# A statically ordered gated-attention kernel: V copies on another engine, gate rows by DMA, a serial-queue model and a split last round

## The chip, the cores and the metric

The kernel runs on one core of one Trainium2 chip. The metric is the device time in microseconds (us) of one execution. The time is a little longer than the span of the profile: the execution before that was profiled has a span of 677.7 us, and the timed runs of it lie near 680.

An exponential takes the larger part of the work here, so three engines matter most: ScalarE (ACT in the profile), which computes exponentials; VectorE (DVE) and GpSimd (POOL), which together compute the same function by integer arithmetic for a share of the blocks; and TensorE (PE), which makes the scores and the products with V. SP (SyncE) is the engine that issues nearly all DMAs. PSUM is the memory that holds the results of the matmuls; the kernel uses it in banks of 512 columns.

## The reference, cut to what matters

```python
def reference(A_x, A_wqkv, A_wo, B_x, B_wqkv, B_wo, gate_w):      # S = 2048, D = 512, H = 32, Dh = 16
    x = A_x
    g = _sigmoid((x * gate_w).sum(-1, keepdims=True))
    a = _A_ref(x, A_wqkv, A_wo)     # softmax attention, 32 heads, then @ wo
    b = _B_ref(x, B_wqkv, B_wo)     # linear attention with phi(t) = elu(t) + 1, then @ wo
    return g * a + (1 - g) * b
```

Softmax attention over 32 heads of 2048 x 2048 scores, with a head size of only 16, makes 134 million exponentials. That is why the exponential, not the matmul arithmetic, sets the scale of the time.

## The kernel before

The kernel writes its instructions in an order that it computes itself while it is built. It has a list scheduler: each candidate instruction has a planned duration, a priority and a set of reads and writes; at each step the scheduler takes the best candidate, and some twenty constants ("weights") decide what is best. The result is one fixed order per engine, with semaphore waits worked out from the reads and writes. I call the length that this computation expects for its own order "the plan". It is a number of the builder, not a time.

The waits are put on an instruction in the order in which the dependencies happen to be listed:

```python
def add(self, fn, deps=(), inc=True, dma_sem=None):
    waits = []
    for d in deps:
        if d is None:
            continue
        ...                                  # keeps the highest value for each semaphore
        waits.append((sem, val))
```

The scores are 2048 blocks of 128x512. ScalarE takes two at a time (128x1024). VectorE takes single blocks by one add and clamp (`op1`), and each pair of such blocks then needs two shifted copies, on GpSimd or on VectorE:

```python
return C(AC, 500, 427 * n + 49, lambda: nc.scalar.activation(              # pair of blocks on ScalarE
    P[:, slot, 0:512 * n], bank(b0, n), ACT.Exp, scale=ESC), ...)
return C(DV, OPP, 533 * n + 74, lambda: nc.vector.tensor_scalar(o, i, ZB, 0.0, op0=ALU.add, op1=ALU.max), ...)   # op1
if E is PO and (len(dst["shifts"]) < PMIN or PO.free > DV.free + PLATE): ...  # GpSimd leaves the shift
    return C(PO, 400, 70 + 484 * n, lambda: nc.gpsimd.tensor_tensor(...), ..., f"pshift {m}")
return C(DV, ..., 69 + 134 * n, lambda: nc.vector.tensor_scalar(...), ..., f"shift {m}", lock=True)
```

How many blocks go to VectorE isn't a constant. A rule hands out one block, or two if VectorE has little queued and fewer than SHB shifts wait:

```python
got = sorted(got[:min(len(banks[:2]) if len(dst["op1"]) < 1 and DV.free < start + BACK
                      and len(dst["shifts"]) < SHB else 1, cur["todo"])])
```

The three shifted terms of such a block need V scaled by three coefficients: V itself and two scaled copies of it, made on GpSimd after VectorE has cast V out of PSUM:

```python
yield dv(607, lambda: nc.vector.tensor_copy(Vc[:, 0, vs, :, :, 0:16], src), [r_bank[b]], [r_V[vs]])
for k in range(1, NTERM):
    yield po(690, lambda k=k: nc.gpsimd.tensor_scalar(Vc[:, k, vs]..., Vc[:, 0, vs]..., COEF[k], 1.0,
                                                      op0=ALU.mult, op1=ALU.mult), [r_V[vs]], [r_V[vs]])
```

The gate is spread over partitions by four tiny VectorE copies (`dv(150, ... nc.vector.tensor_copy(gnat[32*a:32*(a+1), :], src))`). A DMA is planned as "start plus latency", whatever else its queue holds:

```python
start = max(E.free, _avail(E, reads, writes))
E.free = start + issue                # issue = 60
fin = start + lat
```

The output of each attention round is transposed, normalised, and transposed back as `OAT` in whole 128x512 pieces; after the last round the projection and four output copies follow.

The softmax here doesn't subtract the row's maximum and nothing guards it: scores larger than these inputs give would overflow.

## Time and profile before

| | before |
|---|---|
| time, median of three runs | 680.0 us (679.25 to 680.65) |
| span of the profiled execution | 677.7 us |
| ScalarE: pairs and singles of exponentials | 694 + 1 |
| first exponential starts | 9.93 us |
| last exponential starts / span ends | 668.73 / 677.71 us |
| ScalarE stalls between first and last exponential | 16.0 us |
| blocks on VectorE | 659 |
| shifts on GpSimd / on VectorE | 465 / 195 |

The stalls come from the trace by one rule: for each exponential, take the distance from its start to the start of ScalarE's next instruction, and subtract the normal step (904 ns for a pair, 477 ns for a single and for one of the 32 `phi` activations). What is left over is stall. Busy shares can't give this, because ScalarE's recorded spans overlap. The prediction below shows the profile lines themselves.

### The profile page before, as it was taken

What the parts mean: (1) busy time and instruction counts of PE and PEld (TensorE: products, weight loads), DVE (VectorE), ACT (ScalarE), POOL (GpSimd) and SP (SyncE); (2) the same over time, 40 slices, a digit from 0 to 9 for tenths busy, and PEclk for the clock granted to TensorE, in tenths of its full rate; (3) what the DMA queues carried; (4) which work ended last, traced back from release to release, by engine and by line L of the source; (5) the groups of instructions that cost most, each with busy time, mean ns of one, the idle gap of its engine ahead of it and who ended that gap; (6) DMA issues with size and microseconds to landing.
All of it is one profiled execution on the core that took longest, in us unless ns stands there. A gap on an engine that the chain in (4) does not pass through costs nothing.

```text
span 677.7 us, 24102 instructions
## 1 busy us (share of the span) xinstructions
PE 667.5 (98%) x9886; PEld 203.2 (30%) x9886; DVE 607.9 (90%) x1062; ACT 658.2 (97%) x734; POOL 550.1 (81%) x611
## 2 busy tenths in 40 slices
PE   8999999999999999999999999999999999999998
PEld 4322233323223232222333322232332332222222
DVE  6999999998899998999899888899998988899996
ACT  5899999999999999999999999999999999999995
POOL 3767878888878888888897888898788997887882
PEclk9999999999999999999999999999999999999999
DMA  6430001200000000000002000001020021000000
GB/s 133 135 89 8 4 2 35 69 9 3 2 10 1 10 2 2 10 2 2 12 3 65 10 10 1 10 18 22 7 34 9 14 48 31 17 16 11 26 17 32
DMA packets 27963, 15.96 MB, mean 24 GB/s; under 512 B 19792, under 2 KB 26832, under 8 KB 27856
## 3 DMA queue, kind: packets, MB, share of 16 engines
q1 hardware_dynamic: 26512, 13.91, 8.1%
q8 instruction: 79, 1.29, 0.8%
q10 hardware_dynamic: 1344, 0.52, 0.3%
q14 instruction: 28, 0.23, 0.1%
HBM read 6.69 MB, written 2.10 MB: 13 GB/s over the span
## 4 chain that ended last, share of the span: by engine, by line
PE 77%; ACT 13%; issue 5%; DVE 4%; DMA 0%; POOL 0%; ACTq 0%; DVEq 0%; POOLq 0%
PE ps L371 59%; PE ps L377 18%; ACT P L771 11%; DVE Z L685 2%; ACT eb L1056 1%; DMA xnat<-wA 0%; DVE T L1021 0%; DVE gnat L1013 0%; DVE QT L957 0%; DVE wA L1163 0%; PE ps L899 0%; DVE Z L749 0%; DVE OAT L1048 0%; POOL Z L739 0%; DVE rec L1040 0%
## 5 line engine op out<-in xcount | busy, mean ns | idle before, releaser
L771 ACT ACTIVATE P<-ps 128x1024 bf16<-128x1024 f32 x695 | 645.6, 1118 | 5.9 <-PE ps L371 5.8
L739 POOL TENSOR_TENSOR Z<-Z,mcon 128x512 int32<-128x512 int32 x465 | 480.0, 1056 | 81.9 <-DVE Z L685 49.4
L685 DVE TENSOR_SCALAR Z<-ps 128x512 int16<-128x512 f32 x659 | 441.2, 684 | 53.3 <-PE ps L371 45.7
L371 PE MATMUL ps<-Z,Vc 128*17 128x512 bf16 x1977 | 282.4, 382 | 0.2
L371 PE MATMUL ps<-Qz,KT 32*128 32x512 bf16 x2048 | 272.2, 384 | 3.4 <-DVE Z L685 1.0
L371 PE MATMUL ps<-P,Vc 128*17 128x512 bf16 x1389 | 250.1, 383 | 0.2
L371 PEld LDWEIGHTS ps<-Qz,KT 32*128 32x128 bf16 x2048 | 68.5, 91 | 259.1 <-ACT P L771 235.1
L371 PEld LDWEIGHTS ps<-Z,Vc 128*17 128x17 bf16 x1977 | 63.8, 88 | 79.4 <-issue 52.3
L749 DVE TENSOR_SCALAR Z<-Z 128x1024 int16<-128x1024 int16 x195 | 81.2, 433 | 0.2
L371 PEld LDWEIGHTS ps<-P,Vc 128*17 128x17 bf16 x1389 | 56.3, 88 | 55.4 <-issue 40.7
L371 PE MATMUL ps<-warm 128*32 128x512 bf16 (+15 forms) x600 | 62.5, 327 | 1.2 <-DVE dummy L420 1.2
L377 PE MATMUL ps<-xT,wA 128*32 128x512 bf16 (+1 forms) x528 | 43.9, 376 | 0.1
L1057 POOL TENSOR_SCALAR eb<-eb 128x512 f32<-128x512 f32 x32 | 20.1, 629 | 15.6 <-ACT eb L1056 9.1
L988 POOL TENSOR_SCALAR Vc<-Vc 128x576 bf16<-128x576 bf16 x32 | 21.6, 675 | 6.9 <-DVE Vc L985 3.5
L371 PEld LDWEIGHTS ps<-warm 128*32 128x32 bf16 (+1 forms) x600 | 20.3, 96 | 18.8 <-issue 12.4
L1021 DVE STREAM_TRANSPOSE T<-ps 128x512 f32<-128x512 f32 x32 | 22.6, 708 | 2.5 <-PE ps L377 2.3
L377 PE MATMUL ps<-wA,xnat 128*32 128x512 bf16 x256 | 22.6, 382 | 1.7 <-DVE wA L1163 1.7
L1044 POOL TENSOR_TENSOR T<-T,rg 128x256 bf16<-128x256 f32 x31 | 19.5, 630 | 5.7 <-DVE Z L749 2.7
L377 PE MATMUL ps<-phiK,xnat 128*32 128x512 bf16 x256 | 23.1, 383 | 0.0
L377 PE MATMUL ps<-wA,OAT 128*32 128x512 bf16 x256 | 22.5, 382 | 0.0
L1056 ACT ACTIVATE eb<-ps 128x512 f32<-128x512 f32 x32 | 22.5, 702 | 0.0
L377 PE MATMUL ps<-wB,xT 128*32 128x512 bf16 x256 | 22.4, 381 | 0.0
(79 smaller groups left out, 279.2 us busy)
## 6 DMA issues: line engine op xcount, KB each, us to landing
Qz<-QT SPq DMA_DIRECT2D x120, 16.0 KB, 1.8
wA<-in_A_wqkv_dram SPq DMA_DIRECT2D x4, 384.0 KB, 4.6
wB<-in_B_wqkv_dram SPq DMA_DIRECT2D x4, 384.0 KB, 3.3
xnat<-in_A_x_dram SPq DMA_DIRECT2D x3, 512.0 KB, 3.7
out_dram<-outt SPq DMA_DIRECT2D x12, 128.0 KB, 1.7
wA<-in_A_wo_dram SPq DMA_DIRECT2D x1, 512.0 KB, 3.6
wA<-in_B_wo_dram SPq DMA_DIRECT2D x1, 512.0 KB, 4.6
out_dram<-wA SPq DMA_DIRECT2D x4, 128.0 KB, 1.8
```

The costliest lines, as they stand in the source:

```text
L371: return lambda: nc.tensor.matmul(o, lhsT=l, rhs=r, start=start, stop=stop, skip_group_check=sg)
L377: h = nc.tensor.matmul(o[32 * j:32 * j + 32], lhsT=l[:, 32 * j:32 * j + 32], rhs=r, start=start, stop=stop, skip_group_check=True)
L685: return C(DV, OPP, 533 * n + 74, lambda: nc.vector.tensor_scalar(o, i, ZB, 0.0, op0=ALU.add, op1=ALU.max), [r_bank[b] for b in bks], r_Z[ ...
L739: return C(PO, 400, 70 + 484 * n, lambda: nc.gpsimd.tensor_tensor(Z[:, z, 0:512 * n].bitcast(I32), Z[:, z0, 0:512 * n].bitcast(I32), mcon[ ...
L749: return C(DV, 450 if hot else 300, 69 + 134 * n, lambda: nc.vector.tensor_scalar(Z[:, z, 0:512 * n], Z[:, z0, 0:512 * n], float(m), None, ...
L771: return C(AC, 500, 427 * n + 49, lambda: nc.scalar.activation(P[:, slot, 0:512 * n], bank(b0, n), ACT.Exp, scale=ESC), [r_bank[b0 + k] fo ...
L988: yield po(690, lambda k=k: nc.gpsimd.tensor_scalar(Vc[:, k, vs].rearrange("p a b c -> p (a b c)"), Vc[:, 0, vs].rearrange("p a b c -> p ( ...
L1021: yield dv(607, lambda: nc.vector.transpose(T1[:, a, :], bank(7)), [r_bank[7]], [r_T1[a]])
L1044: yield E(340 if r == NR - 1 else 640, lambda k=k: (nc.vector if r == NR - 1 else nc.gpsimd).tensor_tensor(dst_[:, k], src[:, k, :, 0:16], ...
L1056: yield ac(480, lambda: nc.scalar.activation(eb[:, i, :], bank(b), ACT.Exp), [r_bank[b]], [r_eb[i]])
L1057: yield po(640, lambda: nc.gpsimd.tensor_scalar(eb[:, i, :], eb[:, i, :], 1.0 + 1e-6, 0.0, op0=ALU.min, op1=ALU.max), [r_eb[i]], [r_eb[i]])
```

## The change

The intent is to shift load between VectorE and GpSimd, to take small delays off single places, and to make the plan agree better with the chip, with the weights searched anew for the new plan. The core of it, cut:

```diff
@@ add: the wait expected last is placed first
-        for d in deps:
-            if d is None:
-                continue
+        for d in sorted([d for d in deps if d is not None], key=lambda d: -d.fin if isinstance(d, _Ev) else 0.0):
@@ weights (some of them)
-    SHB = 4
+    SHB = 3
-    PMIN = 2
+    PMIN = 1
-    SLK = 43.219
+    SLK = 88.975
...
@@ serial queue model in dma(); occ is 1100 for transposes and loads, 650 otherwise
+            if E is SP and occ:
+                q_free[0] = max(q_free[0], start) + occ
+                fin = q_free[0] - occ + lat
@@ V copies
-                yield po(690, lambda k=k: nc.gpsimd.tensor_scalar(Vc[:, k, vs]..., COEF[k], 1.0, op0=ALU.mult, op1=ALU.mult), ...)
+                yield ("OP", DV, 214, lambda k=k: nc.vector.tensor_scalar(Vc[:, k, vs]..., COEF[k], None, op0=ALU.mult), ..., True)
@@ gate rows
-                yield dv(150, lambda a=a, src=src: nc.vector.tensor_copy(gnat[32 * a:32 * (a + 1), :], src), [r_ge], [r_gnat])
+                yield ("DMA", gnat[32 * a:32 * (a + 1), :], gp[32 * a:32 * (a + 1), 16 * a:16 * (a + 1)], semGN, 64, 2500.0, ...)
@@ last round in halves of 256 columns
+            if r == NR - 1:
+                for hf in range(2):
+                    ...        # transpose, reciprocal, gate, multiply, transpose back, each on half the columns
+                    yield ("FLAG", lambda hf=hf: flags.add(("oatl", hf)))
+                return
@@ the last projections wait for their own half; three of the four last copies on ScalarE
-            yield ("WAIT", lambda: ("oat", NT8 - 1, qc) in flags)
+            yield ("WAIT", lambda: (("oatl", qbl // 2) if tail else ("oat", NT8 - 1, qc)) in flags)
-            if tail and qbl % 2 == 1:
+            if tail and qbl != 2:
```

## The prediction

> **What bounds the kernel now.** I read the page's busy line first, then the groups by line, then the start-to-start spacing of each engine's instructions in the trace, then the waits, and last the timeline around each hole of ScalarE. The busy line and five groups (line, engine, operation, names, shapes, count | busy us, mean ns | idle before, releaser):
>
> ```profile
> PE 667.5 (98%) x9886; PEld 203.2 (30%) x9886; DVE 607.9 (90%) x1062; ACT 658.2 (97%) x734; POOL 550.1 (81%) x611
> ...
> L771 ACT ACTIVATE P<-ps 128x1024 bf16<-128x1024 f32 x695 | 645.6, 1118 | 5.9 <-PE ps L371 5.8
> L739 POOL TENSOR_TENSOR Z<-Z,mcon 128x512 int32<-128x512 int32 x465 | 480.0, 1056 | 81.9 <-DVE Z L685 49.4
> L685 DVE TENSOR_SCALAR Z<-ps 128x512 int16<-128x512 f32 x659 | 441.2, 684 | 53.3 <-PE ps L371 45.7
> ...
> L749 DVE TENSOR_SCALAR Z<-Z 128x1024 int16<-128x1024 int16 x195 | 81.2, 433 | 0.2
> ...
> L988 POOL TENSOR_SCALAR Vc<-Vc 128x576 bf16<-128x576 bf16 x32 | 21.6, 675 | 6.9 <-DVE Vc L985 3.5
> ```
>
> There are 2048 score blocks of 128x512. ScalarE takes them in pairs by its exponential (694 pairs and one single: 1389 blocks). The other 659 go to VectorE (L685, one each), with one 1024-wide shift per block, 465 of them on GpSimd (L739) and 195 on VectorE (L749). Spans of ScalarE overlap (1118 ns long, yet typically 904 ns from start to start), so its 97% hides stalls. By spacing, ScalarE's floor is 694 x 0.904 + 32 x 0.477 (phi, L1056) + about 0.9 (one single, one gate) = 643.6 us. The first exponential starts at 9.9 us and the last is over at about 669.6, so 659.7 us hold 643.6 of work: **ScalarE is the bound, with 16 us of stalls, a head of 10 us and a tail of 8 us**. Time can fall only through fewer exponentials (0.904 us a pair), fewer stalls, or a shorter tail.
>
> Summing what each start-to-start step exceeds its normal step by gives where the 16 us are: 3.7 between 20 and 40 us, 0.9 at 65 us, 1.8 at 559 us, the other 9.5 or so spread thin. The timeline (start us, us, engine, instruction) names three causes:
>
> ```profile
> 22.48 1.42 POOL L988 TENSOR_SCALAR Vc<-Vc 128x576 bf16<-128x576 bf16 x2
> 24.23 0.40 PE L371 MATMUL ps<-P,Vc 128*17 128x512 bf16 x4
> 24.68 1.02 ACT L771 ACTIVATE P<-ps 128x1024 bf16<-128x1024 f32 x1 [1.42 <-PE ps L371]
> ...
> 63.12 2.13 DVE L1013 COPY gnat<-ge 32x16 f32<-32x16 f32 x4
> 66.76 1.94 ACT L771 ACTIVATE P<-ps 128x1024 bf16<-128x1024 f32 x2 [0.76 <-PE ps L371]
> ...
> 556.36 5.19 SPq L348 DMA_TRANSPOSE xnat<-wA  x3
> 559.63 0.69 DVE L1163 TENSOR_TENSOR wA<-ps,wA 128x512 bf16<-128x512 f32 x1 [2.06 <-DMA xnat<-wA]
> 561.50 1.02 ACT L771 ACTIVATE P<-ps 128x1024 bf16<-128x1024 f32 x1 [1.66 <-PE ps L371]
> ```
>
> First: PV matmuls stand behind the scaled V copies on GpSimd, and ScalarE starves. Second: four tiny gate copies, planned at 150 ns each, hold VectorE 2.13 us. Third: eight Qz copies and three transposes queue on SyncE's in-order queue, which the build-time scheduler took for independent, so VectorE stands 2.06 us at an instruction issued too early. The tail:
>
> ```profile
> 670.41 0.72 DVE L1021 STREAM_TRANSPOSE T<-ps 128x512 f32<-128x512 f32 x1 [2.27 <-PE ps L377]
> 672.12 0.71 DVE L1048 STREAM_TRANSPOSE OAT<-T 128x512 bf16<-128x512 bf16 x1
> 672.88 1.20 PEld L377 LDWEIGHTS ps<-wA,OAT 128*32 128x32 bf16 x28 [0.42 <-DVE OAT L1048]
> 674.63 0.59 ACT L1202 CAST wA<-ps 128x512 bf16<-128x512 f32 x1 [0.49 <-PE ps L377]
> ```
>
> From the accumulator's transpose to OAT is 2.4 us in series, then 2.4 us of projection and copies, then 2.5 us of output DMA.
>
> **What the Trainium skill says.** "SBUF — State Buffer", section "Who interferes with whom": VectorE in a 2-port mode and GpSimd exclude each other for a whole instruction. The trace agrees: the gate copies last 167 to 969 ns for one shape, the shifts L749 283 to 1160 ns. "VectorE: DVE Perf Modes", section "Mode 4×_2P": a bf16 tensor_scalar from SBUF to SBUF may make 4 elements a cycle. The shifts agree in slope: 434 ns for 1024 elements, 284 for 512, so 0.29 ns an element. "Perfetto Trace Analysis", section "Identifying Dependency Chains": an instruction that waits on several engines may have EventSemaphore instructions ahead of it. The trace shows them, and the wait that the source places first is the one left on the instruction. From release to start I find 51 ns on TensorE when the last release was for the instruction's own wait, 115 ns when it was for the separate one; on GpSimd (VectorE releasing) 79 against 149.
>
> **Part by part.**
>
> V copies. GpSimd loses 32 x 0.75 us (spacing) = 24.0 us. It can take 24.0 / 0.995 = 24 more shifts, worth 24 x 0.331 = 8.0 us of VectorE. VectorE gains 32 copies; from the two shift shapes one of 576 elements lasts 303 ns and, with the shifts' overlap of 103 ns, takes 0.20 us: 6.4 us. Net gain 1.6 us of VectorE, **almost a wash**. The port time is a wash too (24 us of GpSimd traded for shifts there). What remains is latency: V ready after 0.5 us instead of 1.42, off the hole at 22 to 26 us (2.2 us): I take 1.2 us.
>
> Gate rows by DMA: 2.1 us of VectorE off, and the 0.9 us hole at 65 us. Four small DMAs join the queue at about 0.7 us each (as the Qz ones do), long before the rows are first used at 449 us.
>
> VectorE work: 1.6 + 2.1 = 3.7 us freed; a block moved from ScalarE costs it 0.598 + 0.331 = 0.93, so 4 blocks, 2 exponentials, 1.8 us.
>
> Thresholds (shift queue 4 to 3, GpSimd may take a lone shift, PMIN 2 to 1, and the searched weights): GpSimd idles 81.9 us before its shifts and VectorE 53.3 us before L685. If a tenth to a fifth of GpSimd's idle turns into shifts (8 to 16), VectorE gains 2.7 to 5.3 us; with better use of its own gaps I put 8 more blocks, 4 exponentials, 3.6 us. This is a choice, not a derivation.
>
> Wait order: some 100 waits on TensorE end with a separate semaphore instruction last, 64 ns each, so 6.4 us of TensorE; some 45 on GpSimd at 70 ns, 3.2 us. Most is beside ScalarE's work. Of the thin 9.5 us I take 2.0.
>
> DMA queue model: the hole at 559 us, 1.8 us.
>
> Last round in halves: first half's OAT comes about 1.3 us after the accumulator instead of 2.4 (two 341 ns transposes as planned, small ops between), the second about 0.2 us later than now; half the projection and its copies then lie under the second half. After OAT I expect 1.2 us instead of 2.4, so net 1.0 us.
>
> Sum: 1.2 + 0.9 + 1.8 + 3.6 + 2.0 + 1.8 + 1.0 = 12.3 us. The whole order is made anew, so new accidents like those at 34, 37 and 369 us (0.3 to 0.6 us each) will come; I charge 3.3 us. 680.0 - 12.3 + 3.3 = **671 us**.
>
> **Rivals.** (a) Resource wash: ScalarE keeps about 695 exponentials and only the named holes and the tail go, less accidents: 675 to 679. For it: VectorE and GpSimd merely exchange work, TensorE has no slack to show. (b) The engines get fuller: lone shifts let GpSimd use a third of its idle time, exponentials fall by 15 to 20, and the time to 658 to 664. For it: 82 us idle on GpSimd and 53 on VectorE; against it: those gaps are mostly waits for L685 and for TensorE, so for data. (c) Port collision: 32 more 2-port operations wait up to 0.8 us each for a GpSimd shift, up to 20 us of VectorE and a time of 680 to 688; against it, the copies carry the scheduler's lock flag, unlike the gate copies.
>
> **Range and chances.** I hold (a) at 30%, the middle path at 50%, (b) at 15%, (c) at 5%. Two per cent faster is below 666.4 us: it needs (b) or a lucky middle, 0.18. Slower by 2% is above 693.6: 0.02. Range 663 to 678.
>
> **What would show it.** Right: Vc copies on VectorE near 300 ns; exponentials near 689 (count of L771); no hole above 1 us on ScalarE between 40 us and its last exponential; GpSimd shifts up by 20 or more and VectorE shifts down; separate-semaphore releases last on TensorE falling from 100 to a few tens; last OAT to last output copy near 1.2 us. Wrong: a count of L771 below 680 (then the thresholds mattered more), an unchanged count with new holes (then (a)), or Vc copies of 0.6 us and more (then (c)).

## The result and the profile after

| | before | after |
|---|---|---|
| time, median (range), 4 runs each in the same rounds | 680.33 us (679.25 to 682.12) | 676.80 us (676.61 to 677.12) |
| span of the profiled execution | 677.7 us | 674.8 us |

The ratio is 0.9946, with a 95% interval of 0.9924 to 0.9968. A ratio here is always the mean time of one kernel's fast runs over the mean of the other's fast runs of the same rounds, so it isn't quite the ratio of the medians quoted. The kernel is 3.5 us faster by the medians; the forecast was 9.0 us. The time lies inside the predicted range of 663 to 678 us, near its slow end. All outputs are right.

The page of the kernel after gives the busy line and the groups that answer to those of the prediction (line, engine, operation, names, shapes, count | busy us, mean ns | idle before, releaser):

```profile
PE 662.7 (98%) x9908; PEld 201.6 (30%) x9933; DVE 602.8 (89%) x1066; ACT 658.2 (98%) x735; POOL 556.8 (83%) x604
...
L778 ACT ACTIVATE P<-ps 128x1024 bf16<-128x1024 f32 x695 | 645.6, 1138 | 4.6 <-PE ps L377 4.3
L746 POOL TENSOR_TENSOR Z<-Z,mcon 128x512 int32<-128x512 int32 x490 | 508.0, 1061 | 82.4 <-DVE Z L692 61.1
L692 DVE TENSOR_SCALAR Z<-ps 128x512 int16<-128x512 f32 x658 | 441.7, 684 | 57.3 <-PE ps L377 51.6
...
L756 DVE TENSOR_SCALAR Z<-Z 128x1024 int16<-128x1024 int16 x168 | 69.4, 427 | 0.1
```

Its groups by line also have the weight loads of the score matmuls (PEld, which overlaps with the matmuls) and the V copies:

```profile
L377 PEld LDWEIGHTS ps<-Qz,KT 32*128 32x128 bf16 x2048 | 67.6, 90 | 262.0 <-ACT P L778 234.3 <-DVE Z L692 15.9 <-issue 5.1
...
L995 DVE TENSOR_SCALAR Vc<-Vc 128x576 bf16<-128x576 bf16 x32 | 9.9, 311 | 0.1
```

Work did move as intended: GpSimd has 25 more shifts (465 to 490), VectorE 27 fewer (195 to 168), and each V copy lasts 311 ns. But the count in L778 did not move: 695 pairs, against 694 pairs and one single. VectorE's busy time fell by 5.1 us (607.9 to 602.8), and its idle time before its block instruction rose by 4.0 us (53.3 to 57.3). The freed time became idle time.

Next, the two named holes in the timeline (start us, us, engine, instruction; a number in brackets at the end is idle time before it). Around the gate and around 559 us after the change:

```profile
59.48 7.69 ACT L778 ACTIVATE P<-ps 128x1024 bf16<-128x1024 f32 x8
62.07 2.41 SPq L358 DMA_DIRECT2D gnat<-ge  x4
```

```profile
539.32 23.19 ACT L778 ACTIVATE P<-ps 128x1024 bf16<-128x1024 f32 x25
541.41 8.07 SPq L354 DMA_TRANSPOSE xnat<-wA  x4
552.13 4.96 SPq L358 DMA_DIRECT2D Qz<-QT  x8
555.61 0.65 DVE L1190 TENSOR_TENSOR wA<-ps,wA 128x512 bf16<-128x512 f32 x1
```

ScalarE runs through both places in one unbroken row of exponentials, 8 and 25 of them. Before the change, three of the eight transposes stood behind the Qz copies in the queue, and a VectorE instruction waited for the first of these. Now six stand before the Qz copies (the four shown are the last of them) and two behind, at 557.13 and 558.99 us, but no VectorE instruction waits for those two: the last of its kind, at 555.61 us, starts without a wait.

At the start there is a new hole (timeline after):

```profile
13.95 3.03 POOL L746 TENSOR_TENSOR Z<-Z,mcon 128x512 int32<-128x512 int32 x3 [2.23 <-DVE Z L692]
15.35 0.68 DVE L992 CAST Vc<-ps 128x512 bf16<-128x512 f32 x1
17.14 0.30 DVE L995 TENSOR_SCALAR Vc<-Vc 128x576 bf16<-128x576 bf16 x1
17.30 1.04 POOL L746 TENSOR_TENSOR Z<-Z,mcon 128x512 int32<-128x512 int32 x1 [0.32 <-DVE Z L692]
18.62 0.30 DVE L995 TENSOR_SCALAR Vc<-Vc 128x576 bf16<-128x576 bf16 x1
20.03 0.60 PE L377 MATMUL ps<-P,Vc 128*17 128x512 bf16 x6
20.47 6.52 ACT L778 ACTIVATE P<-ps 128x1024 bf16<-128x1024 f32 x7 [1.88 <-PE ps L377]
```

V is cast by 16.03 us, and its two copies, 0.30 us each, are over only at 18.92 us: one starts 0.16 us after a GpSimd shift has ended (16.98), the other 0.28 us after the next one (18.34). ScalarE waits 1.88 us.

And the tail (timeline after):

```profile
667.52 0.45 DVE L1031 STREAM_TRANSPOSE T<-ps 128x256 f32<-128x256 f32 x1 [3.89 <-PE ps L377]
668.77 0.45 DVE L1059 STREAM_TRANSPOSE OAT<-T 128x256 bf16<-128x256 bf16 x1
669.14 0.41 DVE L1031 STREAM_TRANSPOSE T<-ps 128x256 f32<-128x256 f32 x1
670.35 0.45 DVE L1059 STREAM_TRANSPOSE OAT<-T 128x256 bf16<-128x256 bf16 x1
671.95 0.58 ACT L1229 CAST wA<-ps 128x512 bf16<-128x512 f32 x1 [1.15 <-PE ps L383]
```

The halves do what they say, but a half transpose takes 0.41 to 0.45 us where a whole one took 0.72, so two halves in series are longer than one whole.

The span, taken apart by the stall rule:

| part of the span (us) | before | after | predicted change | measured change |
|---|---|---|---|---|
| first exponential starts | 9.93 | 9.31 | 0 | -0.62 |
| stalls up to 40 us | 3.84 | 4.65 | -1.2 | +0.81 |
| hole at 65 us (gate copies) | 0.91 | 0 | -0.9 | -0.91 |
| hole at 559 us (queue) | 1.77 | 0 | -1.8 | -1.77 |
| other stalls | 9.5 | 9.06 | -2.0 | -0.4 |
| exponentials | 694 + 1 | 695 | -5.4 | 0 |
| last exponential's start to the end | 8.98 | 8.97 | -1.0 | -0.01 |
| "new accidents" | | | +3.3 | in the rows above |
| sum | 677.71 | 674.78 | -9.0 | -2.9 |

The kernel before ends on a single exponential and the kernel after on a pair, so the row of the tail compares unlike ends; from the start of the accumulator's first transpose to the end it is 7.30 us before and 7.26 us after, which says the same. This is one profile of each kernel, so a row below about 0.5 us is not worth much. A second profile of the same kernel after (run a_again below) has a span of 676.6 us, 1.8 us more: its first exponential starts at 9.85, and it has a hole of 1.1 us near 22 us that the first profile lacks, before which TensorE waited for DMA transposes of x. The two large rows that vanished, 65 and 559 us, are absent in both (at 545 us the second has two stalls of 0.34 and 0.26).

### The profile page after: what moved, and what is told of

Same layout as the page of the kernel before. It is cut to its first block, busy times and chain, and to the rows that moved or that the text cites. A ratio compares the mean times of both kernels' runs of the same rounds, so it can differ in the third digit from the quotient of the medians.

```text
span 674.8 us, 24186 instructions
## 1 busy us (share of the span) xinstructions
PE 662.7 (98%) x9908; PEld 201.6 (30%) x9933; DVE 602.8 (89%) x1066; ACT 658.2 (98%) x735; POOL 556.8 (83%) x604
## 4 chain that ended last, share of the span: by engine, by line
PE 48%; ACT 37%; issue 13%; DVE 1%; DMA 1%; ACTq 0%; DVEq 0%
PE ps L377 37%; ACT P L778 36%; PE ps L383 10%; ACT eb L1083 1%; DMA xnat<-wA 1%; DVE Z L692 0%; DVE T L1035 0%; ACTq L1495 0%; PE ps L906 0%; DVE wA L1190 0%; ACT wA L1229 0%; DVE T L1031 0%; DVE OAT L1059 0%; ACT KT L930 0%; DVE Z L756 0%
## 5 line engine op out<-in xcount | busy, mean ns | idle before, releaser
L778 ACT ACTIVATE P<-ps 128x1024 bf16<-128x1024 f32 x695 | 645.6, 1138 | 4.6 <-PE ps L377 4.3
L746 POOL TENSOR_TENSOR Z<-Z,mcon 128x512 int32<-128x512 int32 x490 | 508.0, 1061 | 82.4 <-DVE Z L692 61.1
L692 DVE TENSOR_SCALAR Z<-ps 128x512 int16<-128x512 f32 x658 | 441.7, 684 | 57.3 <-PE ps L377 51.6
L377 PE MATMUL ps<-Z,Vc 128*17 128x512 bf16 x1974 | 275.3, 382 | 1.7 <-DVE T L1035 1.4
L377 PE MATMUL ps<-P,Vc 128*17 128x512 bf16 x1390 | 244.2, 383 | 0.0
L377 PEld LDWEIGHTS ps<-Qz,KT 32*128 32x128 bf16 x2048 | 67.6, 90 | 262.0 <-ACT P L778 234.3
L377 PEld LDWEIGHTS ps<-Z,Vc 128*17 128x17 bf16 x1974 | 61.4, 88 | 76.1 <-issue 50.4
L377 PEld LDWEIGHTS ps<-P,Vc 128*17 128x17 bf16 x1390 | 54.3, 88 | 55.5 <-issue 45.1
L756 DVE TENSOR_SCALAR Z<-Z 128x1024 int16<-128x1024 int16 x168 | 69.4, 427 | 0.1
L377 PE MATMUL ps<-warm 128*32 128x512 bf16 (+14 forms) x624 | 60.0, 327 | 4.6 <-issue 3.2
L383 PE MATMUL ps<-xT,wB 128*32 128x512 bf16 x256 | 22.0, 382 | 0.0
```

The source lines that it names most:

```text
L377: return lambda: nc.tensor.matmul(o, lhsT=l, rhs=r, start=start, stop=stop, skip_group_check=sg)
L383: h = nc.tensor.matmul(o[32 * j:32 * j + 32], lhsT=l[:, 32 * j:32 * j + 32], rhs=r, start=start, stop=stop, skip_group_check=True)
L756: return C(DV, 450 if hot else 300, 69 + 134 * n, lambda: nc.vector.tensor_scalar(Z[:, z, 0:512 * n], Z[:, z0, 0:512 * n], float(m), None, ...
```

## The experiments

Twelve kernels ran. A name that starts with b is the kernel before with something added, a is the kernel after with something undone or added, n is a new set of weights. The runs of the kernel before beside them had medians of 680.95, 680.84 and 680.75 us in the three groups.

These runs of the kernel before are of two kinds. In the first group 5 have a granted TensorE clock of 1.000 in the mean and a mean time of 680.46 us, and 6 have 0.997 and 681.34 us; in the third group 4 have 1.000 (680.29 us) and 5 have 0.997 (681.40 us). The ratios mix them. b_sort, b_halves and b_gate_same, which keep the old order, have runs at 0.997 too; every run of a kernel whose plan knows the queue has 0.999 or 1.000.

### First group: one part alone on the kernel before

**b_dma: the serial queue model alone.** The weights stay as they were; the plan makes a new order.

```diff
+            if E is SP and occ:
+                q_free[0] = max(q_free[0], start) + occ
+                fin = q_free[0] - occ + lat
...
-            yield ("DMA", dst, src, sem, 16 * n, lat, [now()], wr, False, k == 0)
+            yield ("DMA", dst, src, sem, 16 * n, lat + 1000.0, [now()], wr, False, k == 0)
```

> The kernel before with the serial DMA queue model alone, and with its own old weights; the order is made anew from about two thirds of the run on. The theory of the parts: the hole at 559 us closes, 1.8 us less, 678.5. The rival: the order that this model makes is longer in itself (its builder expects 1.1 us more than for before), so that the hole goes but no more than 0.7 us is gained, or the hole is only moved.

Measured: 678.94 us (678.64 to 679.63), ratio 0.9972 (0.9960 to 0.9983). The timeline around the old hole:

```profile
544.16 31.31 ACT L774 ACTIVATE P<-ps 128x1024 bf16<-128x1024 f32 x34
...
560.07 0.68 DVE L1166 TENSOR_TENSOR wA<-ps,wA 128x512 bf16<-128x512 f32 x1
```

The hole is gone, 34 exponentials run through it, and the time falls by about 2 us. This confirms that part: forecast 1.8 us, measured 1.9 (0.28% of 680.95). All five runs have a clock of 1.000; against the runs of the kernel before with the same clock it is 1.5 us by the means (678.99 against 680.46), so about 0.4 us of the 1.9 are the kernel before's runs at the lower clock. The new plan was in fact 1.1 us longer than the old one, and still the chip was faster: the old plan was shorter only because it didn't know of the queue.

**b_gate_same: gate rows by DMA, order unchanged.** The four VectorE copies become four memsets of one column that keep their slots in the order, and four DMAs are issued.

```diff
-                yield dv(150, lambda a=a, src=src: nc.vector.tensor_copy(gnat[32 * a:32 * (a + 1), :], src), [r_ge], [r_gnat])
+                yield dv(150, lambda a=a: nc.vector.memset(dummy[:, 0:1], 0.0), [r_ge], [r_dummy])
+            def rows():
+                for a in range(4):
+                    dma(SP, gnat[32 * a:32 * (a + 1), :], gp[32 * a:32 * (a + 1), 16 * a:16 * (a + 1)], semGN, 64, 2500.0, ...)
```

> The kernel before with the gate rows by four small DMAs alone; in the plan the four copies are replaced by four tiny memsets, so that every compute engine keeps its order. Both theories: the hole at 65 us closes (0.9 us less), time about 679.4. If the hole had another cause, it stays and the time is unchanged.

Measured: 681.07 us, ratio 1.0003 (0.9990 to 1.0016). No gain. Yet the hole at 65 us is gone from its profile. What is there instead, in that profile's timeline, lies 490 us later:

```profile
559.45 0.69 DVE L1171 TENSOR_TENSOR wA<-ps,wA 128x512 bf16<-128x512 f32 x1 [1.82 <-DMA xnat<-wA]
561.32 1.97 ACT L772 ACTIVATE P<-ps 128x1024 bf16<-128x1024 f32 x2 [1.47 <-PE ps L371]
```

Stalls of 1.59, 1.04 and 0.51 us stand at 559, 562 and 564 us where the kernel before has one of 1.77, and one of 0.82 at 503 us where it has none above 0.15. Two things other than the gate rows go into that. The stall at 503 us (a VectorE instruction that waits for a transpose) stands also in the profiles of b_dma (0.81) and b_sort (0.59), which don't have the gate edit. And the longer stalls from 559 us on go with a lower clock. From `--windows` of this run (stretch, its length, busy us of PE, PEld, DVE, ACT and POOL, then the granted clock, the DMA share and GB/s):

```profile
561.00:564.00 3.00, 3.00 (x29) 0.60 (x26) 1.70 (x3) 1.97 (x2) 1.58 (x2) 0.66 0.24 49
```

In the next 3 us the mean is 0.78. The trace's clock records have it at half from 561.94 us for 3.4 us. The profile of b_halves has the same from 560.36 us, with stalls of 2.52, 0.61 and 0.27 there; the profiles of the kernel before and of b_sort, with the hole but at full clock, don't. All five runs of b_gate_same have a clock of 0.997; against the six runs of the kernel before at 0.997 the means are 681.12 and 681.34, so 0.2 us is gained in place of the 0.9 that was forecast. What brings the clock down isn't shown, and why the saving was lost on this order stays open: the stall at 503 us, the clock and a start of the run with 0.7 us more stall (4.57 us up to 40 us, against 3.84) are all candidates.

**b_dma_gate (second group): both together.** Edit: the two above in one kernel.

> The kernel before with the queue model (678.9 us in the first call, few runs apart) and the gate rows by DMA, whose four copies are replaced by tiny memsets so that every compute engine keeps its order. If the hole of 0.9 us at 65 us is on the path to the end, 0.9 us less than with the queue model alone: 678.0 or a ratio to before of 0.9958. If it was absorbed later, as the run on the old order suggests, no change: 0.997.

Measured: 677.94 us (677.15 to 678.16), ratio 0.9957 (0.9943 to 0.9972). On the order without the 559 us hole, the same gate edit is worth 1.0 us (678.94 to 677.94, in two groups on one chip), as forecast (0.9). The ranges of the times don't overlap; the intervals of the two ratios do. Part of it may be the stall of 0.81 at 503 us in the profile of b_dma, which that of b_dma_gate lacks. These two parts together give 2.9 us of the 3.5 us.

**b_halves: the last round in halves.** Edit: the halves of the change in `aout`, the two flags and the choice of copies, nothing else.

> The kernel before with the last round in halves alone; the order up to the last round is the one of before. The theory of the parts: 1.0 us less, 679.3. The rival (the halves' fixed costs eat what the overlap gives, as the two tails of 8.98 and 8.97 us suggest): 0.0 within 0.2 us, and the span from the start of the accumulator's transpose to the end stays at 7.3 us.

Measured: 680.73 us (678.48 to 682.05), ratio 0.9990 (0.9975 to 1.0006). From the last exponential's start to the end it takes 8.90 us, against 8.98: no gain worth the name. The profiled execution had an unusual hole at its start, which explains what the hole near 22 us is (timeline of b_halves):

```profile
18.59 0.58 SPq L352 DMA_DIRECT2D gwc<-in_gate_w_dram  x1
...
21.80 1.05 PE L378 MATMUL ps<-xT,wA 128*32 128x512 bf16 x16 [0.62 <-DMA xT<-in_A_x_dram]
22.04 0.61 POOL L995 COPY T<-gwc 128x512 bf16<-128x512 bf16 x1 [1.53 <-DMA gwc<-in_gate_w_dram]
22.74 1.71 POOL L989 TENSOR_SCALAR Vc<-Vc 128x576 bf16<-128x576 bf16 x2
...
24.50 0.40 PE L372 MATMUL ps<-P,Vc 128*17 128x512 bf16 x4 [0.84 <-POOL Vc L989]
24.95 1.02 ACT L772 ACTIVATE P<-ps 128x1024 bf16<-128x1024 f32 x1 [3.02 <-PE ps L372]
```

The V copies stand behind the gate-weight copy in GpSimd's order; that copy waits for a DMA which is issued only at 18.59 us, behind the transposes of x; TensorE itself waits for one of those. The hole that I had charged to the V copies' duration, 1.54 us in the kernel before, is 3.14 us here, although all engines have the same instructions in the same order up to there. So DMA landings move it by as much as its own size.

**b_sort: only the order of the waits.**

```diff
-        for d in deps:
-            if d is None:
-                continue
+        for d in sorted([d for d in deps if d is not None], key=lambda d: -d.fin if isinstance(d, _Ev) else 0.0):
```

> The kernel before with the sorted waits alone; every engine's order of instructions is the one of before. The theory of the parts (the prediction): about 2.0 us less, 678.3, and the releases by a separate semaphore instruction nearly gone. The theory of the holes (the gain comes from the two holes of ScalarE at 65 and 559 us alone): the holes stay, at 0.9 and 1.8 us, and the time falls by 0.0 to 0.7 us. If the earlier start of the first exponential after the change (9.31 us in place of 9.93) comes from the wait order, it shows here too.

Measured: 679.93 us (679.09 to 681.57), ratio 0.9989 (0.9976 to 1.0003). The interval holds 1: at best this part is worth 1.6 us, and the midpoint is 0.7 us.

### Second group: parts taken from the kernel after

**a_nosort: the old wait order back.** Edit: `for d in deps:` as before.

> The changed kernel with the waits in their old order; every engine's order of instructions stays. The prediction's size for the wait order: 2.0 us more, 678.8. The theory formed after the first call (where the sorted waits alone gave 0.8 us on the old order, with an interval that just holds zero): 0.3 to 1.2 us more, 677.1 to 678.0, with the thin stalls of ScalarE up by that much.

Measured: 676.99 us (676.78 to 677.06), ratio 0.9941 (0.9927 to 0.9956). Against 676.80 and 677.26 for the kernel after itself, nothing is lost. Both sizes, 2.0 and 0.3 to 1.2 us, missed. The waits did change as meant: on GpSimd, counting its instructions with both kinds of wait that it stood idle for and that VectorE released last, a separate semaphore instruction was the last to be released 40 times before the change and 2 times after it (46 in a_nosort), and the instruction's own wait 28 and 101 times (39 in a_nosort). It is worth nothing that I can measure.

**a_nohalves: the whole last round back.** Edit: `aout` and the last projections as before.

> The changed kernel with the last round whole; order unchanged up to the last round. The prediction: 1.0 us more, 677.8. The rival (halves hide nothing, as their ten small operations cost nearly what the five whole ones do each): 0.0 to 0.2 us more, with the same 7.3 us from the accumulator's transpose to the end.

Measured: 678.08 us (677.46 to 679.46), ratio 0.9961 (0.9948 to 0.9974). By the ratios that is about 0.8 us slower than a_again, and by the medians 1.1 us slower than a_nosort of the same rounds, without overlap of the times. The number is near the prediction's 677.8, but the tail isn't where it lies: from the last exponential's start to the end it is 9.06 us against 8.97. The rest of its difference is earlier in the profile (first exponential at 10.05 us, a hole at 25 us, and two of about half a us at 458 and 545 us), in instructions that the edit doesn't touch, and the intervals of the ratios overlap. So the halves give 0.1 us by the tails; where the rest comes from is not shown.

**a_V2: a second, useless instruction on VectorE beside each V copy.** It is meant to measure what VectorE's time is worth; since it stands just before the V copy, it makes V later too.

```diff
+                yield ("OP", DV, 214, lambda k=k: (nc.vector.tensor_scalar(scr[:, next(rot) % 3, :], Vc[:, 0, vs]...[:, 0:288], COEF[k], None, op0=ALU.mult),
+                    nc.vector.tensor_scalar(Vc[:, k, vs]..., COEF[k], None, op0=ALU.mult))[1], ...)
```

> The changed kernel with a second, useless copy of 288 columns beside each of the 32 scaled V copies on VectorE, not known to the plan, so that every order stays. About 0.15 to 0.2 us each, 5 to 6 us of VectorE in all. If VectorE's time bounded the kernel (the prediction's exchange of freed VectorE time for blocks), 5 us more, 681.8. If VectorE has idle time that no block fills (57 us before its score blocks), less than 1.5 us more, and that in the first 40 us.

Measured: 678.81 us (678.16 to 679.60), ratio 0.9969 (0.9956 to 0.9982). From its groups by line:

```profile
L998 DVE TENSOR_SCALAR scr<-Vc 128x288 bf16<-128x288 bf16 x32 | 7.5, 236 | 0.1
L999 DVE TENSOR_SCALAR Vc<-Vc 128x576 bf16<-128x576 bf16 x32 | 11.4, 355 | 0.0
```

The order is the same, VectorE's busy time is 4.5 us more than after the change (607.3 against 602.8; the 7.5 us of the extra group overlap in part with their neighbours), and the kernel lost 1.8 us against a_nosort of the same group, 1.5 us against a_again. Neither forecast (5 us, or less than 1.5) was met. So a us of unplanned VectorE work at this place costs 0.3 to 0.4 us of time. In the profile 1.2 us of it stand as stalls in the first 40 us (5.94 us, against 4.72 in a_nosort), and V is ready 3.68 us after its cast instead of 3.35. So this run can't tell VectorE's time from V's lateness; it only shows that VectorE's time isn't passed on in full. That it costs time to add work doesn't mean that it saves time to remove it, as the counts above show.

### Third group

**a_again: the kernel after, unchanged.** It gives the run-to-run scale.

> The changed kernel once more, unedited, to compare within the same rounds and to see what one profile differs from another of the same program. 676.8 us within 0.3; first exponential, tail and stalls of ScalarE as before within 0.5 us, or, if DMA landings vary from load to load, up to 1.5 us apart.

Measured: 677.26 us (676.59 to 678.47), ratio 0.9950 (0.9938 to 0.9963); the first measurement was 0.9946. That is 0.2 us outside the 0.3 that I had allowed around 676.8, and its profile has 1.3 us more stall than the first (15.0 against 13.7), within the wider of the two forecasts.

**a_Vpool: the V copies back on GpSimd.** Edit: the old `po(690, lambda k=k: nc.gpsimd.tensor_scalar(...))` in the kernel after, with everything else of the change; a new order.

> The changed kernel with the scaled V copies back on GpSimd and the order made anew; its builder expects an order 0.8 us longer than for the changed kernel. The prediction: moving them is worth about 2.0 us (1.2 of latency and 0.8 of exponentials), so 678.8. The rival, from the trace of after, where V is ready 3.35 us after its first copy in place of 1.80: the move as such is worth nothing, the time is 677.6 (the 0.8 of the order), and V is ready within 2 us again.

Measured: 678.12 us (677.48 to 678.52), ratio 0.9960 (0.9948 to 0.9973): 0.9 us slower than a_again by the medians, with overlapping intervals, and between the two forecasts. It has 696 pairs of exponentials, one more. Each V copy lasts 675 ns again, and yet V is ready sooner: the mean over the 16 V tiles, from the end of the cast to the end of the last copy, is 1.92 us. In the kernel after it is 3.35 us (3.32 in a_again), in the kernel before 1.80 us. The copies are shorter on VectorE, and V comes later.

**a_oldw: the change with the weights of before.** Edit: all weights and DMIN set back.

> The changed kernel with all weights and thresholds of the kernel before (shift queue 4, lone shifts on GpSimd not allowed, minimum 3) and the order made anew; its builder expects 2.8 us more than for the changed kernel. The prediction (thresholds and weights bring 4 exponentials, 3.6 us): 680.4 and 4 exponentials more. The rival (the weights change no count, they only pick an order that fits the changed durations): count of exponentials within 3 of 695, time 679.6 within 1.

Measured: 679.27 us (678.92 to 679.57), ratio 0.9976 (0.9963 to 0.9990), 2.0 us slower than a_again, with 695 pairs and one single. The search's weights are worth 2 us to the new order, through the order, not through the count of exponentials (one single block's difference). In the profile the loss stands in the tail: from the last exponential's start to the end it takes 10.80 us, against 8.97 in a_again, because this order leaves more of the projections to the end (52 of their matmuls start after the last OAT, against 16 in a_again, and the last two copies wait 1.3 and 2.9 us for them); the stalls before it aren't longer (14.7 against 15.0).

**n_search3: other weights for the kernel after.** I tried some thousands of sets of weights for the shortest plan, and ran the best one. No instruction's content changes, only the order and who takes which block.

```diff
-    SHB = 3
+    SHB = 7
-    BACK = 1043.522
+    BACK = 663.876
-    PVW = 685.579
+    PVW = 2864.784
-    DENS = 0.598
+    DENS = 0.693
...                 # HOT, SLK, STICK, HOLD, BIAS, KEYW, DTOL, TTOL, PLATE, AGE, DSL, FILL, PKR..QR, DMIN as well
```

> The changed kernel with other weights, found by trying some thousands of sets for the shortest order that its own builder expects: 3.9 us shorter than that of the changed kernel. If what the builder expects is worth its face value once the two holes are gone (span minus expectation is 13.4 us after, 13.5 for the old order with queue model and gate rows), 672.9 us within 1.5, faster than both kernels. If the order's length does not carry over, 675 to 679.

Measured: 673.18 us (672.29 to 673.44), ratio 0.9886 (0.9873 to 0.9900). It beats both kernels: 4.1 us less than a_again in the same rounds. From its groups by line:

```profile
L778 ACT ACTIVATE P<-ps 128x1024 bf16<-128x1024 f32 x691 | 641.1, 1099 | 5.1 <-PE ps L377 4.9
...
L692 DVE TENSOR_SCALAR Z<-ps 128x512 int16<-128x512 f32 x666 | 443.2, 683 | 44.3 <-PE ps L377 37.8 <-POOL T L1071 0.2
```

Here VectorE's idle time before its block instruction is 13 us lower than after the change, and VectorE takes 8 blocks more, so ScalarE has four pairs fewer: 4 x 0.904 = 3.6 us of the 4.1. It has 467 shifts on GpSimd and 199 on VectorE, more on VectorE than in either kernel. Its plan is 3.9 us shorter than that of the kernel after, and the chip gave 4.1.

## Why the prediction was right or wrong

**What bounds the kernel: right.** ScalarE's exponentials with stalls, a head and a tail describe every kernel here, and the two clear gains can be read off that account. TensorE, at 98% the obvious rival, has 73 us of filler matmuls in its busy time (groups `ps<-warm` of the kernel before: 62.5 and 10.4 us), while ScalarE's steps at their normal length fill 642.8 of the 658.8 us between its first and last exponential.

**The hole at 559 us, -1.8 us: right.** Measured -1.77 us in the profile, and 1.9 us by b_dma alone.

**The hole at 65 us, -0.9 us: right in size on the new order.** It vanished, and b_dma_gate over b_dma shows 1.0 us. On the old order the same edit gave nothing (b_gate_same), which I hadn't foreseen; there the clock and other stalls differed too, so the reason stays open.

**Freed VectorE time, -1.8 us, and thresholds, -3.6 us: wrong, and this is the step that failed.** These two terms were 5.4 of the 9.0 us. The working said: 3.7 us of VectorE are freed, a block costs VectorE 0.93 us, so four blocks move; and the thresholds would move eight more. The first half held: 27 shifts fewer at 0.331 us and 2.1 us of gate copies less, 6.4 us of V copies more, makes 4.6 us freed, and the profile shows 5.1 us less busy time. The second half did not: not a single block moved, and 4.0 us of the freed time stand as idle before L692. The false link is "freed time on VectorE becomes blocks". How many blocks VectorE gets is decided by the rule that hands one block, or sometimes two, to a score wave when a PSUM bank is free; of the 57.3 us of VectorE's idle time there, 51.6 us end with a matmul. There VectorE waits for TensorE. And TensorE's score matmuls wait in turn for ScalarE to free their banks: ScalarE ended 234.3 of the 262.0 us that the weight loads of the scores stood idle. So blocks are handed out at ScalarE's pace. The builder's log shows it: of the 695 score waves that the kernel after makes for ScalarE, 640 carry one block for VectorE, 9 carry two and 46 none; before, it was 610, 24 and 61. Waves with two became fewer, and SHB, lowered from 4 to 3, is one of the conditions for a second block.

The runs agree with that: putting all the weights back (a_oldw) changed the count by one single block, and the weights of n_search3, which cut the idle time by 13 us, bought 8 blocks. Builds that were never run on the chip say more. With PMIN 2 in place of 1 the kernel after gets the identical order, so the threshold that I bet on does nothing. And no value of SHB from 2 to 8, of BACK from 500 to 3000 or of DMIN from 2 to 5, each changed alone, brought ScalarE's blocks below 1388. GpSimd's idle time before its shifts, of which I expected a tenth to a fifth to be used, went from 81.9 to 82.4 us: GpSimd's 25 extra shifts take the time of the V copies and no more, which is the 24 of the working.

**Latency of V, -1.2 us: wrong in sign.** The duration was right (311 ns, forecast 303). The step "V is ready after 0.5 us" was not: 3.35 us, against 1.80 before. The trace shows in the early hole that each copy starts just after a GpSimd shift has ended, and score blocks are placed between cast and copies. I had used the lock flag (with it, the builder places an instruction of VectorE so that none of GpSimd runs beside it) as a point against the port collision. The copies are short (311 ns in the mean, where the unflagged gate copies took 167 to 969 ns), but they stand later in the order. No run separates the flag from the competing blocks, but the plan does, as far as a plan can: it expects V 3.34 us after the cast, as measured, and a build of the kernel after without the flag on these copies expects 1.52 us (not run; its plan is 2.4 us longer as a whole). So the delay was in the plan, and the flag makes it. Moreover, the hole at 22 to 26 us was not the V copies' alone (b_halves). What the part is worth as a whole is 0.9 us by a_Vpool, at the edge of what these runs resolve, and about what the plan says (0.8 us).

**Last round in halves, -1.0 us: wrong; the mis-sized term is "the second half about 0.2 us later".** Measured from the start of the first transpose, the first OAT comes at 1.70 us (forecast 1.3) and the second at 3.28 us, where the whole one took 2.42: 0.86 us later. From the last OAT to the end of the last copy it took 1.73 us instead of 2.39, against 1.2 forecast, and the output after it 2.25 instead of 2.49. The sum is 0.86 - 0.66 - 0.24 = -0.04, and the step before the first transpose gives 0.03 back. The five small instructions don't halve: 0.45, 0.20, 0.17, 0.29 and 0.45 us for a half, 0.72, 0.25, 0.17, 0.42 and 0.71 us for the whole.

**Wait order, within -2.0 us of thin stalls: mis-sized, nearly all of it.** The thin stalls fell by 0.4 us, and a_nosort shows nothing for this part. The working multiplied some 100 separate waits on TensorE by 64 ns as if they were the awaited ones. My count takes the latest event of each engine as the release, which counts too many; after the change it still gives 77, not "a few tens". Counted again only where nothing of TensorE was still running when the last release came, the kernel before has 2 such waits (104 ns from release to start, against 46 ns in the 4 cases of the other kind) and the kernel after none; the ends of matmuls are modelled, so this is rough. For GpSimd the recount gives the step of the working, 133 against 68 ns in the median.

**One reading.** The shifts "283 to 1160 ns" in the prediction mix two shapes: the wide ones take 407 to 1160 ns, and the two narrow ones 283 and 284. It supports the point all the same.

**Accidents, +3.3 us: not needed.** There was a new one, 2.1 us at 17.5 us, in part the V copies. The other new holes are smaller. Without this charge the forecast would have been further off; it covered part of the error in the exponentials, and that was luck.

**The rivals.** Rival (a), the resource wash with 675 to 679 us, is what happened: the count stayed and the named holes went, less the tail, which I had counted on even there. It had 30%, and the middle path, for which I chose eight blocks without a derivation, had 50%. The evidence that was on the page pointed to (a): the gaps before L685 were waits for TensorE.

**Where the 3.5 us come from.** The queue model and the gate rows give 2.9 us (of which about 0.4 us, as said under b_dma, is that the runs at the lower clock are gone). What is left for the other parts together is 0.6 us, which is about the size of what these runs resolve, so I don't share it out among them. The plan of the kernel after is 0.7 us longer than that of the kernel before (661.4 against 660.7), and the span exceeds the plan by 13.4 us instead of 17.0. So the gain is not a better plan but a plan that the chip follows more closely; a second profile of the kernel after gives 15.2 us for the same excess, so the size of this shift is between 2 and 4 us.

## What to carry to other kernels

Time freed on an engine is worth something only if a rule or a queue turns it into less work for the engine that bounds; before you convert freed time into moved work, read what ends that engine's idle time. In a kernel whose order is fixed at build time, look first for places where the chip departs from the plan (here a DMA queue that the plan didn't know, and 150 ns instructions that took 0.5 us): once the plan knew of these, its length told the time: the orders planned 3.9 us shorter, 0.8 us longer and 2.8 us longer than the kernel after (n_search3, a_Vpool, a_oldw) measured 4.1 us shorter, 0.9 longer and 2.0 longer than a_again. With the plan that didn't know, it had not: b_dma was planned 1.1 us longer and ran 1.9 us faster. Splitting a short serial chain in two pays only if the pieces really get shorter: half a transpose was 0.6 of a whole one.

## What the Trainium skill lacked or had wrong

- "DMA: Bandwidth & Descriptors", section "Issuing engines are not separate DMA queues", calls the time to initiate a DMA "usually small relative to the DMA itself". It isn't here: the eight Qz copies of 16 KB hold the issuing engine for 4.96 us, 0.62 us each, against a median of 1.8 us from issue to landing, and each of the four transposes shown above holds it for 1.2 to 1.7 us (5.4 us in all, within a row of 8.07 us). In the kernel before, such a series of copies and transposes cost 1.8 us of ScalarE's time at 559 us.
- "Perfetto Trace Analysis", section "Identifying Dependency Chains", says that semaphore instructions may stand ahead of an instruction, but not what they cost: from release to start on GpSimd 133 ns against 68 ns in the median, where VectorE releases. Nor does it say that this may not matter: with the old order of the waits the changed kernel still took 676.99 us.
- "ScalarE: Activation LUTs", section "What ACT_TABLE_LOAD costs", has back-to-back activations overlap by about 93 ns. In the kernel before, neighbouring exponentials of 128x1024 overlap by 200 ns in the median (103 to 295 for nine in ten), with spans of 1117 ns and 904 ns from start to start. So a busy share of 97% hid 16 us of stalls, and I found the advice to take start-to-start distances instead for GpSimd alone.
- No page that I read says what an order that keeps VectorE's copies off GpSimd's instructions can lose by it: the V copies kept to 311 ns on VectorE, but V was ready 3.35 us after its cast, against 1.80 us when GpSimd made them at 675 ns each.
- No page that I read warns that two profiles of one and the same program differ by DMA landings: spans of 674.8 and 676.6 us, with a hole of 1.1 us in one that the other lacks.
